# A spectral filter and MLP kernel: the first batch turned on TensorE in SBUF instead of through DRAM, and the stages of the later batches scheduled further ahead

## Chip, cores, metric

One core of one Trainium2 chip. The metric is the device time of one execution in microseconds (us), lower is better. The kernel before: 631.26 us, the median of 3 runs (625.03 to 633.33). Spans of a profiled execution ("the trace") are 1.7 to 2.0 us shorter than the same execution's device time. TensorE does the matmuls; the operand that stays in its array is called the weights, the other one moves. Its results land in the memory PSUM, from which VectorE or ScalarE copies them to the memory SBUF ("evicts" them). GpSimd copies within SBUF, and the DMAs move data to and from DRAM. "Granted clock" is the share of the full TensorE clock that the profile records as granted.

## The reference, cut to what matters

```python
X = np.fft.rfft(x, axis=1)                 # x: 8 batches x 3136 positions x 256 channels
y = np.fft.irfft(X * (filt_r + 1j*filt_i), n=3136, axis=1)
h = y.transpose(0, 2, 1) @ U @ V           # low rank over positions, rank 32
u = y + h.transpose(0, 2, 1)
out = u + np.maximum(u @ w_ch1, 0) @ w_ch2 # w_ch1: 256 x 1024, w_ch2: 1024 x 256
```

The Fourier transform over 3136 = 64 x 49 positions is done as matmuls in two steps with a filter product between the second step and its inverse. Between the steps rows and columns of the 64 x 49 arrangement have to change places.

## The kernel before

Each batch passes through `f1` (first transform), `mid` (second transform, filter product `uv`, its inverse), `low_rank`, and the output stage. An output group is 8 steps of the main loop; a batch is 6 groups or 48 steps. The change of places is done by writing a tile to DRAM (`ct1`, `ct2`) and reading it back in another order.

```python
def f1(u):                                        # cut
    ...   pf = w.T @ x ; asb = pf (evicted) ; store1: asb -> DRAM ct1

def mid(u):                                       # cut
    def do_i1(k, uv):
        pe = ps.tile([128, 2, DM], F32, tag="o" if u.n == 0 else "z", bufs=2)
        ...   pe = gz.T @ uv ; nc.scalar.copy(e, pe) ; e -> DRAM ct2
    for k in range(0, NK, 2):
        if u.n == 0 and i == 0:
            mirror_filters(c)                     # one part of the filters, 4 parts
        ...   a2 = load from ct1
        pz = ps.tile([128, 2, DM], F32, tag="z", bufs=2)
        nc.tensor.matmul(pz, wz[0], a2)
        nc.vector.tensor_mul(uv, pz, fab)
        if len(uvs) > 2: do_i1(*uvs.pop(0))       # 17 steps of this generator
        yield

def low_rank(u):  ...  load e2l and the tiles eb from ct2 ; ph = aus.T @ e

def stage4(gr):   ...  pu = eb.T @ sv ; ut = pu   # starts an output group
def mm1(gr, t):   ...  phh = w1.T @ ut ; h = relu(phh)
def mm2_part(gr, t): . pc += h.T @ w2 ; och = pc ; och -> out

for u in units[1:]:                               # steps, counted over all groups
    s = 48 * u.n                                  # u's own output starts at step s
    deal(f1s[u.n], 7, 2 if first else s - 62, 9 if first else s - 48)
    deal(mids[u.n], 17, 15 if first else s - 44, s - 11)
    for w in (s - 8, s - 6):
        plan[w].append(ranks[u.n])
```

Note for later: for every batch but the first, `pz` and `pe` share the two PSUM buffers of tag "z". The Tile scheduler places the instructions of each engine from this program; TensorE then takes its matmuls in that order: in the waits shown here no later matmul starts before the one that waits (6.6 us, below).

## Time and profile before

| stretch of the trace | us |
|---|---|
| start to the first `ut` eviction (the head) | 84.1 |
| first `ut` of a batch to first `ut` of the next: batches 0 to 6 | 73.5, 70.0, 71.5, 69.0, 65.6, 65.6, 62.3 |
| batch 7, without further transforms | 46.4 |
| last `ut` to the end | 19.5 |
| sum | 627.5 |

The `ut` eviction is the first VectorE instruction of an output group; its 49 start times cut the trace into comparable pieces. These periods are differences of those start times.

The busy tenths of the page in 40 slices of 15.7 us, for TensorE, for the granted TensorE clock and for the DMA engines:

```profile
PE   2145469997999979997999989999999999999996
PEclk9996669999899979999999999999999999999999
DMA  9768939528834587238834596338633663342112
```

TensorE is mostly idle in the first five slices; after that it is busy, with dips (a 7) at about 140, 220, 280 and 360 us.

Waits of TensorE, from the answer that lists who waited for whom (us in total, times, longest):

```profile
PE pu L425 <- DMA eb<-ct: 25.5, 6, 11.8
PE pz L339 <- DMA a<-ct: 17.9, 2, 16.6
PE pz L339 <- DVE uv L348: 13.0, 4, 4.3
```

Of the 25.5 us, 11.8 lie in the head; the other five waits are the dips. The head from VectorE's side, its timeline (start, duration, engine, line, what, how often, and in brackets the idle time before and who ended it):

```profile
35.93 4.62 DVE L348 TENSOR_TENSOR uv<-pz,fab 113x1024 f16<-113x1024 f32 x4 [16.08 <-PE pz L339]
40.58 0.69 DVE L196 COPY fab<-fab 64x2048 f16<-64x2048 f16 x1
44.67 4.62 DVE L348 TENSOR_TENSOR uv<-pz,fab 113x1024 f16<-113x1024 f32 x4 [3.41 <-ACT fab L197]
...
84.06 1.23 DVE L428 CAST ut<-pu 128x1024 f16<-128x1024 f32 x1 [9.79 <-PE pu L425]
```

Here the first batch waits for its own DRAM round trip (16.08 us), for a filter mirror in each quarter (3.41 us), and for the second round trip (9.79 us).

A piece of the period, all engines, lines of middle products and one `phh` only:

```profile
395.80 0.38 PE L339 MATMUL pz<-a,mats 98*128 98x512 f16 x1
...
396.02 0.59 PE L307 MATMUL pe<-uv,mats 113*98 113x512 f16 x2
...
396.65 0.58 ACT L318 CAST e<-pe 98x512 f16<-98x512 f32 x1
...
396.89 0.38 PE L438 MATMUL phh<-ut,w1sb 128*128 128x512 f16 x1
...
397.28 0.38 PE L339 MATMUL pz<-a,mats 98*128 98x512 f16 x1
```

A 512-column matmul at full clock lets the next one start after 0.216 us (`phh` to `phh` elsewhere).

### The profile page before, as it was taken

Reading aid. Unit: us, or ns where it says so; the run is one execution under the profiler, and the core shown is the slowest. Engines: PE = TensorE matmul, PEld = TensorE weight load, DVE = VectorE, ACT = ScalarE, POOL = GpSimd, SP = SyncE. Lnnn points to the kernel's source line nnn. Section 1 sums busy time; section 2 is a strip of 40 time slices with the busy share of each in tenths; the row PEclk is TensorE's granted clock in tenths of the full one; section 3 lists DMA queues with packets and bytes.
Section 4 is the critical chain, followed back from the end, with each engine's and each line's share of the span. In section 5 each row is a group of like instructions: output and inputs, shape, how many; then the busy total and the mean of one; then the engine's idle time right before and its main releaser. Section 6 shows DMA issues by size and latency. Waiting matters only on the chain.

```text
span 627.5 us, 11123 instructions
## 1 busy us (share of the span) xinstructions
PE 548.2 (87%) x4427; PEld 377.8 (60%) x4427; DVE 330.8 (53%) x351; ACT 340.4 (54%) x577; POOL 57.7 (9%) x76
## 2 busy tenths in 40 slices
PE   2145469997999979997999989999999999999996
PEld 1112237655766657665776757667766776677775
DVE  1247424694249543884259552975388536843331
ACT  1225236565555736565556745666566665656663
POOL 6379201000000000000000000000000000000000
PEclk9996669999899979999999999999999999999999
DMA  9768939528834587238834596338633663342112
GB/s 214 168 151 161 197 93 244 168 86 212 200 135 140 135 198 243 86 105 201 223 108 137 136 230 210 100 102 231 216 93 95 195 197 107 100 145 86 68 68 101
DMA packets 76868, 95.51 MB, mean 152 GB/s; under 512 B 6775, under 2 KB 60328, under 8 KB 76816
## 3 DMA queue, kind: packets, MB, share of 16 engines
q1 hardware_dynamic: 67440, 77.49, 39.8%
q0 software_dynamic: 7504, 15.91, 15.9%
q10 hardware_dynamic: 1872, 1.41, 0.7%
q8 instruction: 35, 0.57, 0.4%
q14 instruction: 17, 0.14, 0.1%
HBM read 59.10 MB, written 51.58 MB: 176 GB/s over the span
## 4 chain that ended last, share of the span: by engine, by line
PE 59%; DMA 7%; DVE 4%; ACT 3%; SPq 2%; issue 1%; ACTq 0%; DVEq 0%
PE pc L461 21%; PE phh L438 20%; PE pe L307 6%; PE pz L339 4%; DMA eb<-ct 4%; PE pu L425 3%; PE pc L466 3%; PE pf L254 2%; DMA ct<-e 2%; ACT h L440 2%; SPq L369 1%; DVE asb L269 1%; ACT e L318 1%; DMA e2l<-ct 1%; DVE uv L348 1%
## 5 line engine op out<-in xcount | busy, mean ns | idle before, releaser
L440 ACT ACTIVATE h<-phh 128x512 f16<-128x512 f32 x392 | 232.6, 598 | 161.4 <-PE phh L438 160.2
L461 PE MATMUL pc<-w2sb,h 128*128 128x256 f16 x1568 | 246.4, 275 | 0.0
L438 PE MATMUL phh<-ut,w1sb 128*128 128x512 f16 x784 | 243.7, 386 | 2.9 <-DVE ut L428 1.3
L461 PEld LDWEIGHTS <-h 128*128 128x128 f16 x1568 | 149.7, 98 | 82.1 <-issue 8.4
L348 DVE TENSOR_TENSOR uv<-pz,fab 113x1024 f16<-113x1024 f32 x128 | 153.3, 1220 | 42.6 <-PE pz L339 32.7
L472 DVE COPY och<-pc 128x512 f32<-128x512 f32 x98 | 67.2, 686 | 98.9 <-PE pc L466 96.0
L318 ACT CAST e<-pe 98x512 f16<-98x512 f32 x128 | 74.3, 585 | 76.3 <-PE pe L307 75.5
L438 PEld LDWEIGHTS <-w1sb 128*128 128x128 f16 x784 | 95.7, 146 | 18.8 <-issue 8.7
L428 DVE CAST ut<-pu 128x1024 f16<-128x1024 f32 x49 | 59.9, 1223 | 85.5 <-PE pu L425 85.3
L307 PE MATMUL pe<-uv,mats 113*98 113x512 f16 x240 | 77.3, 406 | 0.0
L339 PE MATMUL pz<-a,mats 98*128 98x512 f16 x120 | 47.3, 405 | 32.6 <-DMA a<-ct 17.9
L425 PE MATMUL pu<-sv,eb 96*128 96x64 f16 x768 | 36.2, 196 | 26.0 <-DMA eb<-ct 25.5
L425 PEld LDWEIGHTS <-eb 96*128 96x128 f16 x768 | 32.9, 99 | 40.5 <-issue 24.9
L466 PE MATMUL pc<-idn,ut 128*128 128x128 f16 x392 | 54.8, 221 | 0.0
L307 PEld LDWEIGHTS <-mats 113*98 113x98 f16 x240 | 30.5, 133 | 36.4 <-issue 25.7
L145 POOL DMA_DIRECT2D x<-in_x_dram x24 | 14.5, 626 | 340.7 <-PE pf L254 336.8
L466 PEld LDWEIGHTS <-ut 128*128 128x128 f16 x392 | 38.4, 98 | 9.1 <-issue 0.2
L254 PE MATMUL pf<-x,wf 128*128 128x256 f16 x192 | 33.0, 299 | 11.9 <-DMA x<-in_x_dram 11.7
L269 DVE CAST asb<-pf 128x1024 f16<-128x1024 f32 x21 | 25.7, 1224 | 21.0 <-PE pf L254 18.6
L365 DVE COPY eb<-h 32x2048 f16<-32x2048 f16 x32 | 19.9, 678 | 30.6 <-ACT h L398 30.6
L254 PEld LDWEIGHTS <-wf 128*128 128x128 f16 x192 | 18.7, 104 | 22.3 <-issue 13.6
L267 ACT CAST asb<-pf 128x1024 f16<-128x1024 f32 x21 | 21.2, 1012 | 15.8 <-DMA ct<-asb 7.6
(59 smaller groups left out, 133.5 us busy)
## 6 DMA issues: line engine op xcount, KB each, us to landing
out_dram<-och SPq DMA_DIRECT2D x48, 512.0 KB
ct<-e SPq DMA_DIRECT2D x64, 196.0 KB
x<-in_x_dram POOLq DMA_DIRECT2D x24, 512.0 KB, 6.7
eb<-ct SPq DMA_DIRECT2D x96, 128.0 KB
a<-ct SPq DMA_DIRECT2D x28, 392.0 KB
ct<-asb SPq DMA_DIRECT2D x42, 256.0 KB
a<-ct SPq DMA_DIRECT2D x4, 441.0 KB
ct<-asb SPq DMA_DIRECT2D x3, 288.0 KB
```

The lines of the kernel that those rows point to most:

```text
L254: nc.tensor.matmul(pf[:, (j if u.n == 0 else 2 * i + j), :], w, u.x[c][:, r, :], start=True, stop=True, skip_group_check=True)
L307: nc.tensor.matmul(pe[0:98, :, :], gz[0][f], uv[:, f, :, :], start=(f == 0), stop=(f == 1))
L318: nc.scalar.copy(e[:, i:i + 2, :], pe[0:98, :, :])
L339: nc.tensor.matmul(pz, wz[0], a2[c][:, i:i + 2, 0:DM], start=True, stop=True)
L348: nc.vector.tensor_mul(uv.rearrange("p f k d -> p f (k d)"), zin, fin)
L425: nc.tensor.matmul(pu[:, dh, 64 * i:64 * i + 64], e2[:, s, 128 * dh:128 * dh + 128], sv[:, 64 * r:64 * r + 64], start=(i == 0), stop=True, ...
L428: nc.vector.tensor_copy(gr.ut.rearrange("p h (c q s) -> p h c q s", q=64, s=2), pu.rearrange("p h (c s q) -> p h c q s", q=64, s=2))
L438: nc.tensor.matmul(ph, w1v[:, dh, :, t], gr.ut[:, dh, :], start=(dh == 0), stop=(dh == 1))
L440: nc.scalar.activation(h, ph, RELU)
L461: nc.tensor.matmul(o, gr.h[tt][:, i * 128:(i + 1) * 128], w2sb[:, tt * DM:(tt + 1) * DM], start=(tt == 0), stop=False, skip_group_check=True)
L466: nc.tensor.matmul(o[:, dh * 128:dh * 128 + 128], gr.ut[:, dh, i * 128:i * 128 + 128], idn, start=False, stop=(dh == 1), skip_group_check= ...
L472: nc.vector.tensor_copy(gr.och[:, 2 * y:2 * y + 2, :], gr.pc.rearrange("p (j d) -> p j d", j=2))
```

## The change

Intent: (1) the first batch computes its first transform channel-major (x is the stationary operand), so that the change of places can be done by matmuls against an identity (`turn1`, `turn2`) and stays in SBUF; its filters are all loaded at once, mirrored by three engines, and its rank sum is taken in the spectrum. (2) The stages of batches 2 to 7 come earlier: first transform by 16 to 18 steps, middle transform and rank step by 12.

The diff, cut to its core (`...` and "cut" mark what is left out):

```diff
+    xh = [sb.tile([128, NR, 64], F16, tag="och", bufs=2) for _ in range(2)]   # channel-major
+    uh = cst.tile([128, 2, 100, NK], F16)
+    for c in range(3): ...                                  # first transform, batch 0
+        nc.tensor.matmul(pf[:, j], u0.x[c][:, r, 128*dh:128*dh+128], wf[:, ...])
+        dst = xh[dh][:, 0:48].rearrange("p (h r) k -> p r h k", h=2)[:, r:r + 4]
+        (nc.scalar.copy if n_pf % 2 else nc.vector.tensor_copy)(dst, pf)
+    for c in range(3): ...                                  # the same for U: pu, into xhu
+    def rows_of(t, k):
+        return t.rearrange("p r k -> p (r k)")[:, k:k + 97 * 32 + 1:32]       # 98 columns, 64 bytes apart
+    def turn1(i):                                           # pa = xh turned, 4 matmuls
+        nc.tensor.matmul(pa[0:98, s, ...], rows_of(xh[dh], 2 * i + s), idn)
+        nc.scalar.copy(at[i], pa[0:98])
+    def u_turn(): ... nc.tensor.matmul(pt[0:98, k], rows_of(xhu, k), idn[0:32, 0:32])  # ptu, 32 of them
+    def i1_turned(i): ... nc.tensor.matmul(po[dh][...], uv[:, f, s, ...], gt[...][f])
+        nc.scalar.copy(uh[:, dh, :, 2*i-2:2*i+2], po[dh].rearrange("p k b -> p b k"))
+    def turn2(u, g): ... nc.tensor.matmul(pt[0:96, s, ...], uh[:, dh, b:b + 3]..., idn)  # 100 in all
 # cut: mirrors on VectorE, ScalarE and GpSimd; fab memset moved from GpSimd to VectorE;
 # cut: rank sum h_part from uv; all ct1/ct2 traffic of batch 0 removed
+    for g in range(1, 6):
+        deal(turn2(u0, g), 4, max(8*(g-1)-4, 0), 8*(g-1)+4)
     for u in units[1:]:
         s = 48 * u.n
-        deal(f1s[u.n], 7, 2 if first else s - 62, 9 if first else s - 48)
-        deal(mids[u.n], 17, 15 if first else s - 44, s - 11)
-        for w in (s - 8, s - 6): plan[w].append(ranks[u.n])
+        if u.n == 1: deal(f1s[1], 7, 0, 7); deal(mids[1], 17, 11, 37); rank = (38, 40)
+        else:
+            deal(f1s[u.n], 7, s - 78, s - 66)
+            deal(mids[u.n], 17, s - 56, s - 23)
+            rank = (s - 20, s - 18)
+            x_step[s - 92] = u
```

## The prediction

> **What bounds the kernel now.** Read from the busy times by window: until 84.1 us (the first `ut` eviction) TensorE works about 30 us for the first batch. From the timeline: `x` lands at 8.4 to 15 us; PE then sits idle 16.6 us for the `a` read-back; then four blocks of 8 to 9 us, each gated by a 1.91 us ScalarE filter mirror followed by four 1.15 us `uv` products; then 11.8 us for `eb<-ct`. After 84 us PE is 98 to 99% busy except near 140, 220, 280 and 360 us, where `pu` waits 2.8 to 3.7 us for `eb<-ct` and the granted clock dips afterwards. From one batch's first `ut` to the next's (6 groups): 73.5, 70.0, 71.5, 69.0, 65.6, 65.6 us. So 65.6 us is undisturbed, and some 17 us are lost in the first four: 13 in these waits, the rest mostly at half clock.
>
> **Head after the change.** No DRAM write and read-back, all filter loads queued at once. Estimated: `x` timing unchanged; 96 matmuls of 128 columns end near 19 to 20 us; first `uv` near 23.5 us (it waits for the first ScalarE mirror). Then VectorE is the pacer: 16 products x 1.15 to 1.22 + `aur` 1.2 + two `gb` 2.4 = 23 to 24 us. ScalarE is close behind: 16 `at` x 0.59, 16 `uh` about 0.5, four mirrors x 1.91, three big evictions 1.0 = 28 us from 21 us on. So the last `uv` ends near 47 to 50, then the rest of the inverse, rank sum, first turn, `put_h` and `pu` take 5 to 6 us. First `ut` near 54 us instead of 84: 30 us gained, all on the critical path. GpSimd's mirrors come behind 29 DMA issues of 0.6 us, ready at about 31 us, just in time.
>
> PE in this stage needs about 20 us at full clock but 36 at half. The Trainium skill, "TensorE: Matmul & The Clock Gate", Part 1, says that the array runs at 1.2 GHz until about 3.4 us of sustained activity; the trace agrees (512-column matmuls 0.43 us apart at 36 to 58 us, 0.22 just after). I expect it mostly warm after 30 us.
>
> **Steady part.** Added on PE: 100 turning matmuls of the second transpose. The skill (same page, weight-path perf modes) limits fast weight load to 128-column weights; these have 96: I estimate 0.055 to 0.08 us each, 5 to 8 us in all. Removed: most of the `eb` waits, since the rank step now comes 20 steps ahead instead of 8 (a step is 1.0 to 1.7 us, the loads took 6 to 8 us). Only batch 1 stays tight: its middle transform still ends at step 37 and its tiles are needed at step 44. I leave 8 us of residual waits and half clock of the 17.
>
> **Sum.** 627.5 - 30 - 17 + 8 + 7 = about 595 us in the trace; runs lie about 3 us above it: 598 us.
>
> Chances: faster over 2%: 0.95; within 2%: 0.04; slower: 0.01. Range 584 to 612.
>
> **Signs.** First `ut` at 50 to 59 us; batch periods near 66 us from the second on; the first 75 or more; no `pu<-eb` waits after batch 1; VectorE over 80% busy between 24 and 48 us; clock near full from 30 us.
>
> **What would make it wrong.** PE staying at half clock through the head (+10 us); ScalarE's 64-byte-strided `uh` writes costing much over 0.5 us; the GpSimd mirrors or filter loads arriving late; batch 1's round trips stalling more than 8 us.

## The result

The changed kernel takes 598.61 us, median of 4 runs (594.02 to 600.38), against 629.55 us of the kernel before (4 runs): ratio 0.950, 95% interval 0.941 to 0.959. A ratio here is the mean time of one kernel's fast runs over the mean of the other's fast runs of the same rounds, so it is not quite the ratio of the medians quoted beside it. Executions over 1.5% slower than the fastest of the same kernel are left out of the means. The total is within 1 us of the prediction. The pieces are not:

| stretch | before | predicted | after |
|---|---|---|---|
| head, to first `ut` | 84.1 | 54 | 73.4 |
| first `ut` to the end | 543.5 | 541 | 524.2 |
| of it: batch 0 | 73.5 | 75 or more | 83.1 |
| batches 1 to 6 | 70.0, 71.5, 69.0, 65.6, 65.6, 62.3 | near 66 | 60.3, 63.4, 63.5, 63.5, 63.4, 60.1 |
| span of the trace | 627.5 | 595 | 597.6 |

(541 is 595 less 54.) The head came out 19 us worse than predicted and the rest 17 us better; the right total is two errors that cancel. The experiments below look for both.

The same views after the change. The busy tenths:

```profile
PE   1698896899999999999999999999999999999996
PEclk9955889799999999999999999999999999999999
DMA  9859058558626974397439763756346642422112
```

TensorE is now busy in the head, but at a granted clock of 5 tenths in two slices; the dips later are gone except one at about 100 us. The waits for DMA of more than 1 us, besides that for x:

```profile
PE pu L251 <- DMA un<-in_moe_U_dram: 5.5, 1, 5.5
PE pz L306 <- DMA a<-ct: 6.6, 1, 6.6
```

The first is in the head, the second is the dip at 100 us. The waits of `pu` for `eball` (the old `eb`), 25.5 us before, are 0.3 us in all. The head from VectorE's side:

```profile
28.02 1.22 DVE L317 TENSOR_TENSOR uv<-pz,fab 113x1024 f16<-113x1024 f32 x1 [3.29 <-ACT fab L206]
33.33 2.36 DVE L317 TENSOR_TENSOR uv<-pz,fab 113x1024 f16<-113x1024 f32 x2 [4.09 <-PE pz L306]
...
53.55 3.56 DVE L317 TENSOR_TENSOR uv<-pz,fab 113x1024 f16<-113x1024 f32 x3 [5.09 <-PE pz L306]
...
73.44 1.23 DVE L561 CAST ut<-pu 128x1024 f16<-128x1024 f32 x1 [0.41 <-PE pu L558]
```

VectorE, predicted as the pacer, waits for TensorE's `pz`. Busy time in the stretch of the middle transform (columns: us, then busy us and count of TensorE, weight loads, VectorE, ScalarE, GpSimd; granted clock; DMA share and GB/s):

```profile
20.00:40.00 20.00, 18.23 (x119) 15.46 (x117) 9.01 (x12) 11.45 (x18) 18.43 (x22) 0.67 0.78 112
40.00:60.00 20.00, 17.42 (x132) 13.36 (x131) 10.43 (x11) 15.72 (x22) 7.50 (x8) 0.59 0.72 135
```

TensorE is busy 35.65 of 40 us (89%), VectorE 19.44 (49%). What TensorE does there, from its timeline:

```profile
33.09 0.80 PE L269 MATMUL pa<-mats,xh 128*98 128x128 f16 x4
...
34.74 2.85 PE L277 MATMUL ptu<-mats,eball 32*98 32x32 f16 x16
...
38.67 0.87 PE L328 MATMUL po<-mats,uv 113*128 113x100 f16 x8
39.34 1.55 PE L269 MATMUL pa<-mats,xh 128*98 128x128 f16 x8
```

The start-to-start times of successive matmuls (medians) are 0.167 us for both `pa` and `ptu`, though one moves 128 columns and the other 32. The clock does not matter to `pa` either: from 44.0 to 47.4 us, at full granted clock, they are still 0.167 us apart. That points to a stream bound by its weight loads (tested below with h1, h2 and h4): `pa` and `ptu` are the two that take their weights from `xh` or `xhu` with 64 bytes between columns. `po`, with contiguous weights, is at 0.081 in the half-clock stretches.

The steady part after the change, the same group of lines as before (from the period of batch 4):

```profile
364.85 0.38 PE L306 MATMUL pz<-a,mats 98*128 98x512 f16 x1
...
365.07 0.60 PE L423 MATMUL pe<-uv,mats 113*98 113x512 f16 x2
...
365.71 0.58 ACT L434 CAST e<-pe 98x512 f16<-98x512 f32 x1 [0.55 <-PE pe L423]
...
367.83 0.38 PE L306 MATMUL pz<-a,mats 98*128 98x512 f16 x1
```

The next `pz` comes 1.5 us after the end of the `e` eviction and starts on time. Call a matmul late when it starts more than 0.09 us after the usual start-to-start time for the width of the matmul in front of it. Per batch, this lateness adds up to 3.7 us before (period of batch 4) and 1.6 us after; the difference is the 2.1 us between 65.6 and 63.5. Of it, 1.5 us are the starts of `pz` (2.1 us before, 0.6 after).

### The profile page after: what moved, and what is told of

It is laid out like the page before. It is cut to its first block, busy times and chain, and to the rows that moved or that the text cites. A ratio compares the mean times of both kernels' runs of the same rounds, so it can differ in the third digit from the quotient of the medians.

```text
span 597.6 us, 11827 instructions
## 1 busy us (share of the span) xinstructions
PE 559.9 (94%) x4775; PEld 407.7 (68%) x4775; DVE 347.3 (58%) x370; ACT 356.8 (60%) x608; POOL 46.5 (8%) x68
## 4 chain that ended last, share of the span: by engine, by line
PE 78%; DMA 8%; ACT 6%; POOL 3%; issue 3%; DVE 2%; SPq 0%; ACTq 0%; POOLq 0%
PE pc L594 26%; PE phh L571 26%; PE pe L423 7%; PE pz L306 4%; PE pu L558 4%; PE pc L599 3%; DMA un<-in_moe_U_dram 2%; PE pf L391 2%; ACT asb L394 2%; DMA x<-in_x_dram 1%; ACT e L434 1%; DMA ct<-al 1%; DMA a<-ct 1%; PE pt L506 1%; PE ph L527 1%
## 5 line engine op out<-in xcount | busy, mean ns | idle before, releaser
L594 PE MATMUL pc<-w2sb,h 128*128 128x256 f16 x1568 | 240.4, 273 | 0.0
L434 ACT CAST e<-pe 98x512 f16<-98x512 f32 x112 | 65.0, 586 | 48.5 <-PE pe L423 47.4
L561 DVE CAST ut<-pu 128x1024 f16<-128x1024 f32 x49 | 59.8, 1221 | 11.1 <-PE pu L558 10.9
L423 PE MATMUL pe<-uv,mats 113*98 113x512 f16 x210 | 62.5, 378 | 0.2
L599 PE MATMUL pc<-mats,ut 128*128 128x128 f16 x392 | 54.1, 220 | 0.0
L306 PE MATMUL pz<-a,mats 98*128 98x512 f16 x105 | 39.4, 383 | 8.0 <-DMA a<-ct 6.6
L558 PEld LDWEIGHTS <-eball 96*128 96x128 f16 x768 | 29.8, 98 | 12.2 <-issue 3.9
L461 DVE COPY eball<-h 32x2048 f16<-32x2048 f16 x34 | 22.1, 680 | 21.8 <-ACT h L488 18.4
L423 PEld LDWEIGHTS <-mats 113*98 113x98 f16 x210 | 25.3, 124 | 12.8 <-issue 5.1
L558 PE MATMUL pu<-sv,eball 96*128 96x64 f16 x768 | 31.6, 194 | 0.7 <-DMA eball<-ct 0.3
L391 PE MATMUL pf<-x,wf 128*128 128x256 f16 x168 | 25.8, 275 | 1.1 <-DVE ut L561 0.3
```

The lines of the kernel that those rows point to most:

```text
L306: nc.tensor.matmul(pz, wz[0], a2, start=True, stop=True)
L391: nc.tensor.matmul(pf[:, j], wf[:, 128 * (8 * c + r):128 * (8 * c + r) + 128], u.x[c][:, r, :], start=True, stop=True, skip_group_check=True)
L423: nc.tensor.matmul(pe[0:98, :, :], gz[0][f], uv[:, f, :, :], start=(f == 0), stop=(f == 1))
L434: nc.scalar.copy(e[:, i:i + 2, :], pe[0:98, :, :])
L558: nc.tensor.matmul(pu[:, dh, 64 * i:64 * i + 64], e2[:, s, 128 * dh:128 * dh + 128], sv[:, 64 * r:64 * r + 64], start=(i == 0), stop=True, ...
L561: nc.vector.tensor_copy(gr.ut.rearrange("p h (c q s) -> p h c q s", q=64, s=2), pu.rearrange("p h (c s q) -> p h c q s", q=64, s=2))
```

## The experiments

In the tables "head" is the first `ut`; "batch 0" and "later" are periods as above. "Ratio" is against the kernel before in the same rounds, with 95% interval. Traced spans are single executions. All results were correct. Throughout, TensorE matmuls are told apart by their PSUM tile.

### The two parts apart: s1_sched_only, s2_turn_only

s1 is the kernel before with this edit:

```diff
-        deal(f1s[u.n], 7, 2 if first else s - 62, 9 if first else s - 48)
-        deal(mids[u.n], 17, 15 if first else s - 44, s - 11)
-        for w in (s - 8, s - 6):
+        deal(f1s[u.n], 7, 2 if first else s - 78, 9 if first else s - 66)
+        deal(mids[u.n], 17, 15 if first else s - 56, s - 11 if first else s - 23)
+        for w in ((s - 8, s - 6) if first else (s - 20, s - 18)):
-            x_step[s - 76 if u.n > 2 else s - 74] = u
+            x_step[s - 92] = u
```

> The kernel before with only the new schedule of batches 2 to 7; the first batch still goes through DRAM. Theory A (the schedule carries most of the gain, because the turned first batch gives its shorter head back in the first period): first ut stays at 84 us, the six-group periods from the second on fall from 70.0, 71.5, 69.0, 65.6, 65.6, 62.3 to about 60 to 64, total about 604 us. Rival B (the recorded prediction: the turning gains about 22 us net, the schedule about 9): about 618 us.

s2 is the changed kernel with the reverse edit for batches 2 to 7.

> The changed kernel with the old schedule of batches 2 to 7. Theory A: first ut at 73 us as in the changed kernel, but the later periods go back to about 70, 71, 69, 65.6, so about 620 us. Rival B: about 606 us.

| kernel | median us | ratio | span | head | batch 0 | batches 1 to 6 |
|---|---|---|---|---|---|---|
| before | 630.0 | 1 | 627.5 | 84.1 | 73.5 | 70.0, 71.5, 69.0, 65.6, 65.6, 62.3 |
| s1 schedule only | 601.44 | 0.955 (0.949 to 0.961) | 600.0 | 85.3 | 74.0 | 59.8, 63.5, 63.5, 63.5, 63.5, 60.1 |
| s2 turned batch only | 629.36 | 0.990 (0.978 to 1.002) | 631.1 | 72.1 | 84.5 | 70.9, 70.7, 71.3, 67.7, 65.6, 62.3 |
| after, both | 598.61 | 0.950 (0.941 to 0.959) | 597.6 | 73.4 | 83.1 | 60.3, 63.4, 63.5, 63.5, 63.4, 60.1 |

Two of the four runs of s2, the profiled one among them, counted as slow; its ratio uses the fast two, its periods are only shown for their pattern. Theory A held: the schedule alone brings almost everything. From s1 to after, the traces lose 11.9 us in the head (85.3 to 73.4) and get 9.1 us back in batch 0 (74.0 to 83.1). The turning nets about 2.4 us of trace, where the prediction had 23 (30 less about 7). Single traces scatter here: s3 and s4 below have the same head and the same batch 1, and their head and batch 0 together are 150.5 and 153.4 us, against 156.5 in after and 159.3 in s1. So the net of the turning lies between 2 and 9 us, far from 23 in any case.

### Where the 2.1 us per period come from: s3_shift8, s4_shift4, s6_f1_late

Three versions of the changed kernel, with only this edit:

```diff
-            deal(f1s[u.n], 7, s - 78, s - 66)    # s6: s - 72, s - 60
-            deal(mids[u.n], 17, s - 56, s - 23)  # s3: s - 52, s - 19   s4: s - 48, s - 15
-            rank = (s - 20, s - 18)              # s3: (s - 16, s - 14) s4: (s - 12, s - 10)
```

> The changed kernel, with the middle transform and rank step of batches 2 to 7 only 8 steps further ahead than before, not 12. A group is 8 steps, so this keeps the old place of the middle transforms within a group. Theory P (the 2.1 us per period by which the undisturbed periods fell, 65.6 to 63.5, come from where in the group the middle transforms fall): periods of 65.6 us and no waits for eball. Rival Q (they come from the longer lead): 63.5 us or close.

> The changed kernel with the middle transform and rank step of batches 2 to 7 only 4 steps ahead of the old place: the new place within the group, but little lead. Theory P: undisturbed periods of 63.5 us, with some waits for eball of 0 to 3 us in the early batches. Rival Q: 65 us or more in undisturbed periods.

| kernel | median us | ratio | undisturbed period | spread of the 17 `pz` | steps from first to middle transform | matmuls late, sum per period |
|---|---|---|---|---|---|---|
| before | | 1 | 65.6 | 24.7 us | 4 | 3.7 us |
| s6 | 610.18 | 0.975 (0.969 to 0.981) | 64.7 | 28.7 | 4 | 2.8 |
| after | 598.61 | 0.950 (0.941 to 0.959) | 63.5 | 32.3 | 10 | 1.6 |
| s3 | 595.13 | 0.946 (0.940 to 0.952) | 63.5 | 33.6 | 14 | 1.6 |
| s4 | 596.11 | 0.945 (0.936 to 0.955) | 62.8 | 41.4 | 18 | 1.1 |

Theory P fell: with the old place in the group (s3) the period stays 63.5. Rival Q, the lead by itself, fell too: with the least lead (s4) the period is the shortest. What orders all five rows is the spread of the middle products, which gave theory R, tested with s6:

> The changed kernel with the first transform of batches 2 to 7 six steps later (steps s-72 to s-60), everything else as it is: only 4 steps between it and the middle transform, as in the kernel before. Theory R (the 2.1 us per undisturbed period come from this distance: with 4 steps the read-back tiles a come late, and the 17 middle products are squeezed into about 25 us where VectorE cannot keep up, which costs TensorE a bubble of about 0.18 us at most pz): periods back to about 65.5 us, pz spread over about 25 us, no eball waits. Rival Q (lead alone): 63.5 us as in the changed kernel. Total by R about 608 us, by Q about 598 us.

R held in direction and a little over half in size: the period went from 63.5 to 64.7, not 65.5, because the products were squeezed into 28.7 us rather than 25. Why the same 4 steps gave 24.7 us in the kernel before stays open. The expectation also named the wrong engine. In the period before, 11 of the 17 `pz` start 0.05 us after an `e` eviction of ScalarE ends, and 4 of them (two counted in both) 0.05 us after a `uv` of VectorE; in s4 none does. `pz` and `pe` take turns in two PSUM buffers, and a `pz` that has to follow closely waits until the other engine has emptied one. So: when the read-back tiles come late in the program, the scheduler puts the 17 products close together, and TensorE loses about 0.17 us at most `pz`. In s4, where most are 2.5 us or more apart, no `pz` is late. That the two PSUM buffers are the reason is read from which eviction ends just before; no run gave `pz` and `pe` separate buffers. The total of s6 also holds waits of 9.0 us for `a<-ct` in batch 0's period (88.6 us), so its total says less than its later periods.

### Batch 0's period: s5_mid1_15

```diff
-            deal(mids[1], 17, 11, 37)
+            deal(mids[1], 17, 15, 37)
```

> The changed kernel with the middle transform of batch 1 starting at step 15 instead of 11 (still ending at 37). Theory: the 6.6 us wait of pz for a<-ct in the first period, which blocks all of TensorE's in-order stream, and the half clock after it go away: first period about 76 us instead of 83, total about 591 us. Rival: the tighter middle transform moves the stall to the VectorE-bound products and the eball loads of batch 1, total within 2 us of 598.

Measured: 591.37 us, ratio 0.945 (0.939 to 0.951); batch 0 76.0 us instead of 83.1. This looks as if the theory held, but the other traces do not bear it out. The wait that is left in s5, then that of s3, which has not this edit, then that of c2 (below), which has it:

```profile
PE pz L306 <- DMA a<-ct: 3.2, 1, 3.2
PE pz L306 <- DMA a<-ct: 2.8, 1, 2.8
PE pz L311 <- DMA a<-ct: 6.4, 1, 6.4
```

In the changed kernel TensorE reached `pz` before the last store of the first transform had landed (7.8 us) and been read back (6.3 us), and everything behind `pz` in its order stood still: 6.6 us, and half clock for some microseconds after. The edit did not move this `pz`: TensorE comes to it 26.9 us after the first `ut` in after and 26.7 us in s5 (26.3 to 27.2 in all traces with the turned first batch). What differs is when the read-back could be issued: 24.4 to 26.1 us after the first `ut` in the traces with a wait under 4 us, 26.3 to 27.1 in the others. Without the edit the wait was 1.8 to 6.7 us and batch 0 took 75.5 to 84.5 us (88.6 in s6, with a second such wait); with it, in s5, c1, c2 and c3, 3.2 to 6.4 us and 75.5 to 79.0 us. The ratio of s5 is that of s3 (0.946) and s4 (0.945). So the wait, with the half clock after it, does make batch 0 longer, but that the four steps shortened it is not shown. The prediction had looked for this batch's stall at the `eball` loads of step 44; there it was 0.3 us.

### The head: h1_contig98, h2_contig128, h4_runs16

h1 stores `xh` as 32 blocks of 98 contiguous columns, so the weights of `turn1` and `u_turn` are read contiguously and the eviction writes scattered elements (cut: the same for `xhu` and the last columns, and the order of `pf`):

```diff
-    xh = [sb.tile([128, NR, 64], ...)]
+    xh = [sb.tile([128, NK, 98], ...)]
-                dst = xh[dh][:, 0:48].rearrange("p (h r) k -> p r h k", h=2)[:, r:r + 4]
+                dst = xh[dh][:, :, 0:96].rearrange("p k (h c) -> p h c k", h=2)[:, :, 2 * r:2 * r + 8]
-        return t.rearrange("p r k -> p (r k)")[:, k:k + 97 * 32 + 1:32]
+        return t[:, k]
```

> The changed kernel with the turned first transform stored so that the weights of the first turn lie contiguous (98 columns side by side instead of 64 bytes apart); the evictions write the stride instead. Theory L (the head is bound by TensorE, which loads the strided weights at 0.17 to 0.18 us each): pa drops from 0.17 to about 0.11 us apart and ptu from 0.18 to about 0.09, 7 us less TensorE time, first ut near 67 us instead of 73.4, total about 592 us. Rival M (the head is bound by DMA landing, mirrors and the ScalarE/VectorE chain): spacing falls or not, first ut stays within 1.5 us of 73.

h2 in addition loads 128 columns each time (30 more, results unused):

```diff
-        return t[:, k]
+        return t.rearrange("p k c -> p (k c)")[:, 98 * k:98 * k + (128 if k < NK - 1 else 98)]
```

> As h1_contig98, but each weight load of the first turn takes 128 columns (30 more, whose results nobody reads), so that fast weight load as the skill states it can apply. Theory L with it: ptu falls further, to about 0.03 to 0.06 us, pa stays at the 0.107 of a half-clock 128-column matmul or falls to 0.056 if the denser stream warms the clock; first ut 62 to 66 us, total 587 to 592 us. Rival M: first ut within 1.5 us of 73. If the column count does not matter, the same as h1_contig98.

| kernel | median us | ratio | head | `pa` us apart | `ptu` us apart | one `xh` eviction on ScalarE |
|---|---|---|---|---|---|---|
| after | 598.61 | 0.950 | 73.4 | 0.167 | 0.167 | 0.6 us |
| h1 | 611.21 | 0.977 (0.970 to 0.985) | 89.5 | 0.107 | 0.084 | 2.5 us |
| h2 | 613.01 | 0.978 (0.971 to 0.985) | 90.2 | 0.106 | 0.027 | 2.5 us |
| h4 | 587.24 | 0.930 (0.924 to 0.936) | 65.1 | 0.080 | 0.026 | 0.5 us |

The `pa` of h4 are a mixture of 0.107 us at half clock and 0.056 at full. h1 and h2 did to TensorE what was expected and lost 16 to 17 us of head all the same, which neither theory had foreseen. The reason is on one line of h1's ScalarE timeline:

```profile
20.24 14.98 ACT L240 CAST xh<-pf 128x512 f16<-128x512 f32 x6
```

The changed kernel's evictions of the same size, from the same view:

```profile
20.34 2.21 ACT L239 CAST xh<-pf 128x512 f16<-128x512 f32 x4
```

2.5 us each against 0.55 (the stretch divided by the count; a single record reads 2.96 and 0.58). The write of single 2-byte elements 196 bytes apart takes about five times as long as runs of 64 elements; the evictions on VectorE went from 0.69 to 2.5 us and more. h4 keeps h2's layout and lets the eviction run in the other order, so that it writes 8 neighbouring elements (16 bytes) and takes the stride on the PSUM side:

```diff
-                dst = ....rearrange("p k (h c) -> p h c k", h=2)[:, :, 2 * r:2 * r + 8]
-                src = pf.rearrange("p h r (j k) -> p h (r j) k", j=2)
+                dst = ....rearrange("p k (h c) -> p h k c", h=2)[:, :, :, 2 * r:2 * r + 8]
+                src = pf.rearrange("p h r (j k) -> p h k (r j)", j=2)
```

> As h2_contig128 (contiguous weights, 128 columns a load), but the evictions of the first transform write 8 neighbouring elements (16 bytes) at a time and read PSUM with the stride instead. Theory L2 (h1 and h2 lost 16 us only because 2-byte writes 196 bytes apart made each eviction 2.5 us instead of 0.6; TensorE's weight loads do bind the head): evictions back at 0.6 to 0.8 us, ptu at 0.03 us and pa at 0.11 us or less, first ut at 63 to 67 us instead of 73.4, total 588 to 592 us. Rival M (TensorE is not what binds the head): evictions at 0.6 to 0.8 us but first ut within 1.5 us of 73. If strided PSUM reads cost as much as the strided writes did: evictions stay at 2 us or more and first ut near 89 us.

```profile
19.91 3.11 ACT L240 CAST xh<-pf 128x512 f16<-128x512 f32 x6
```

0.52 us each, and 0.69 on VectorE as in the changed kernel, so the strided PSUM read is free here. TensorE in h4, where 18 `ptu` take 0.71 us (16 took 2.85):

```profile
31.33 0.71 PE L280 MATMUL ptu<-mats,eball 32*128 32x32 f16 x18
31.97 0.61 PE L272 MATMUL pa<-mats,xh 128*128 128x128 f16 x4
```

Theory L2 held: the head is 8.3 us shorter although x landed 0.8 us later in this trace (first matmul at 9.7 us against 8.9); the evictions and the total came out slightly better than expected. Rival M fell: TensorE did bind the head, through its weight loads. The gain lies wholly after the first `uv`: from there to the first `ut` it is 37.5 us against 45.4. Part of this may be the clock, since h4 was granted full clock for 19.1 us of that stretch and after for 13.7. At equal clock, 17.1 us in both, s4 takes 43.8 us and c2 (which has h4's layout) 37.1, so about 6.7 us are the layout alone.

### All parts, and the rest of the head: c1_all, c2_u_early, c3_warm

c1 is h4 with s5's and s4's schedule.

> h4_runs16 with the middle transform of batch 1 from step 15 and those of the later batches 8 steps later (the places of s4_shift4). If the three parts add up: first ut as in h4_runs16, first period about 76 us, later undisturbed periods 62.8 us: total about 578 to 582 us, faster than both kernels. If the shorter head only moves the wait to the first period (its DMAs start earlier but weights and x land no sooner), the first period grows by what the head lost and the total stays near 586.

c2 is c1 with the loads of `un` and `ul` issued ahead of the last two loads of x, because TensorE's order has U matmuls in the middle of the first transform and stood 4.4 to 5.5 us waiting for `un`.

> c1_all with the two loads of U issued ahead of the last two loads of x, so that the U matmuls, which stand ahead of the last third of the first transform in TensorE's order, no longer hold it up for 5 us. Theory U: first transform ends about 2 us earlier (x itself must still land), first ut near 63 us, total about 580 us. Rival: the mirrors and filter loads set the pace after it, first ut within 0.7 us of 65.0.

c3 is c1 with 16 unneeded matmuls in that gap:

```diff
+        if c == 1:
+            warm = ps.tile([128, 512], F32, tag="w", bufs=1, name="warm")
+            for j in range(16):
+                nc.tensor.matmul(warm, u0.x[1][:, j % 8, 0:128], wf[:, 0:512], ...)
+            nc.vector.tensor_copy(wsb, warm[:, 0:2])
```

> c1_all with 16 matmuls of 512 columns that nobody needs, on data of the second x tile, in the 5 us in which TensorE waits for the third; the scheduler then also puts the U matmuls behind the first transform. Theory W (half clock is a large part of what the head costs over the recorded prediction): matmuls of the last third of the first transform at 0.056 us apart instead of 0.107, first ut at 60 to 62 us. Rival: spacing falls but the ScalarE and VectorE evictions and the filter mirrors pace the head by now; first ut no earlier than in c2_u_early.

| kernel | median us | ratio | head | x landed | head less x | batch 0 |
|---|---|---|---|---|---|---|
| after | 598.61 | 0.950 (0.941 to 0.959) | 73.4 | 8.9 | 64.5 | 83.1 |
| h4 | 587.24 | 0.930 (0.924 to 0.936) | 65.1 | 9.7 | 55.4 | 80.4 |
| c1 | 583.73 | 0.927 (0.922 to 0.931) | 65.0 | 9.6 | 55.4 | 75.5 |
| c2 | 584.23 | 0.931 (0.925 to 0.936) | 63.9 | 9.4 | 54.5 | 79.0 |
| c3 | 579.91 | 0.926 (0.921 to 0.930) | 60.5 | 7.5 | 53.0 | 75.5 |

When the first tile of x lands varies from trace to trace (7.3 to 10.2 us) for reasons outside the edits, so heads are compared from there. Even so they scatter: the six traces with the changed kernel's head (after, s2 to s6) have 62.8 to 67.4 us, and single differences below 5 us of this column show nothing. The part from x to the first `uv` is steadier: 18.1 to 19.1 us in those six, 18.0 in h4, 18.4 in c1, 17.5 in c2 and 15.9 in c3. From the first `uv` on, h4, c1, c2 and c3 are alike (37.0 to 37.5 us).

c1: the head of h4 and the later periods of s4 add up, with 62.8 us in the undisturbed later periods; batch 0 took 75.5 us, which for the reason given under s5 is not to be put down to s5's edit. Its trace is 581.8 us, at the upper end of what was expected, because batch 0 and one later period kept small waits (3.8 us for `a<-ct`, 1.8 for `eball`). c2: the wait for U fell to 0.9 us, but the part up to the first `uv` gained only 0.5 to 0.9 us, no more than the scatter: theory U is not shown, and the total did not move. c3: the last third of the first transform runs at full clock,

```profile
15.82 1.06 PE L233 MATMUL pf<-wf,x 128*128 128x128 f16 x16
```

against 1.87 us for 16 in c1:

```profile
20.38 1.87 PE L233 MATMUL pf<-wf,x 128*128 128x128 f16 x16 [0.18 <-ACT xh L240]
```

and the part from x to the first `uv` is 1.6 us shorter than in c2, where the U wait is nearly gone too. Theory W is right in kind and small in size for this stretch; the first `uv` of c3 then waits 4.0 us for a filter load. The clock falls back to half at about 23 us, when TensorE next waits, so c3 does not test what full clock through the whole head would give. c3 has the lowest median of all, 579.91 us, but its ratio is that of c1 within the noise.

## Why the prediction was right and wrong

**Right in the total, 598.0 predicted and 598.61 measured, by two errors that cancel.** The range and the direction were right. The pieces:

1. *"First `ut` near 54 us instead of 84: 30 us gained"* is wrong: 73.4 us. The step that failed is *"Then VectorE is the pacer"*. The load of strided weights by 64 `pa` and 32 `ptu` stands in none of its terms. Measured, each costs 0.167 us, at half and at full clock alike, 16 us for all 96, where the columns alone would give 64 x 0.107 + 32 x 0.027 = 7.7 us at half clock. h4 removed this and got 9.1 us of head, counted from the landing of x.
2. *"I expect it mostly warm after 30 us"* is wrong: the granted clock was 0.50 at 30 to 40 us and 0.59 on average at 40 to 60 us, with TensorE 87 to 91% busy by the records. The prediction's own list of dangers had "PE staying at half clock through the head (+10 us)". c3 shows some of its cost (1.6 us in the first transform). For the rest the traces give a hint: with the same head, the stretch from the first `uv` to the first `ut` took 49.1 us with 3.4 us at full granted clock (s3), 45.0 to 45.4 with 13.7 (after, s2, s5, s6) and 43.8 with 17.1 (s4), about 0.4 us less for each microsecond at full clock (time before the first recorded change is counted as half, as the spacing of the matmuls says). Drawn out to full clock throughout, this estimate gives some 9 us, but it lies far outside what was measured, and with h4's layout (17.1 to 20.5 us at full clock) no such slope shows.
3. Not foreseen: TensorE's order put U's matmuls before the last third of the first transform (5.5 us wait, but worth at most 0.9 us when taken away in c2, which is within the scatter).
4. Cut at the first `uv`, the 19.4 us are 4.5 before it (28.0 us, predicted 23.5) and 14.9 after it (45.4 us, predicted 30.5). Of the 14.9, h4 took back 7.9, of which the layout alone is about 6.7. Some 7 us after the first `uv` stay open; half clock in the middle transform and the waits of 4 to 5 us before `pz`, still there in h4, are the candidates that the traces show. No run separates them.
5. *"65.6 us is undisturbed"* is wrong, and it is the main step that failed in the other direction. Those periods held 3.7 us of late matmul starts that no idle column shows. The new schedule took 2.1 us out of each (s1, with the old first batch, has the same 63.5), s4 2.8 us. The prediction expected "batch periods near 66 us".
6. *Removed: most of the `eb` waits* was right: 25.5 us became 0.3 us. s2 with the old schedule has 13.8 us of them (in a run counted as slow).
7. *"Only batch 1 stays tight"* was right in the batch and wrong in the place: 6.6 us for `a<-ct` at the start of its middle transform, 0.3 us for its tiles at the end. Whether s5 helped this wait is not shown.
8. *100 turning matmuls at 0.055 to 0.08 us, 5 to 8 us in all*: the 79 pairs of successive records in the trace have a median of 0.057 us, 5.7 us for 100, at the low end. The Trainium skill, "TensorE: Matmul & The Clock Gate", section "Weight-path perf modes — Fast Weight Load (FWL) and DoubleRow", restricts the fast load to 128-column weights. This agrees with h1 and h2 (98 columns 0.084 us apart, 128 columns 0.027), but with 128 moving columns no cost of the load of 96 contiguous columns shows: 0.057 us is what 128 columns take with other weights too (0.056).
9. The share-out of the gain was wrong altogether: the prediction gave the turning about 23 us net (30 less 7) and the schedule about 9; the traces say 2.4 us (s1 to after; 2 to 9 with the scatter) and 27.5 us (before to s1).

## What to carry to other kernels

Two orders of the same work can both show an engine 99% busy and differ by 3%: compare the start-to-start times of its instructions with what they take undisturbed, above all where tiles share a few PSUM buffers, and leave a load issued from DRAM enough steps that its users need not be bunched. Price a transposing matmul by its weight load as well as by its moving columns, and choose the layout so that neither the weight load nor the eviction that produces it goes element by element with a stride (2 bytes in every 64 or 196 here); h4 did both by moving the stride to the PSUM side of the eviction. When a total comes out as predicted, check the pieces before believing the reasons. And before a shorter wait is put down to an edit, look at the same wait in the traces that do not have the edit.

## What the Trainium skill lacked or had wrong

- "Advanced Engine Details and Errata", section "Memory Cachelines", says that SBUF has 16-byte lines and that at least two hits on a line are needed for full speed. The runs agree and give the cost, which the page does not: weight loads of 98 columns with one column per line 0.167 us (at half and at full clock), contiguous 0.084 us (at half clock); evictions writing one 2-byte element per line 2.5 us for 512 elements, in runs of 8 elements 0.52 us. Runs of 4 elements (8 bytes, the `uh` evictions) took 0.49 us for 400 elements, so four hits were enough; two were not tried.
- The same section says of PSUM that non-contiguous patterns slow down matmuls and that every two consecutive elements should be contiguous; it does not say what this means for evictions. For reads of PSUM no such cost showed: 512 elements of 4 bytes, neighbours 128 bytes apart, 0.52 us on ScalarE (h4), against 0.55 us in the changed kernel, and 0.69 us on VectorE in both.
- "TensorE: Matmul & The Clock Gate", section "LDWEIGHTS (loading the stationary operand)", gives columns / 1.2 in ns. At half clock this fits (98 / 1.2 = 82 ns, measured 84). At full clock 96 columns must take no more than the 57 ns measured between the `pt` matmuls, less than the page's 80.
- The same page, Part 1, has the clock rise after about 3.4 us of sustained activity. In the changed kernel TensorE was busy without a gap in the records from 30 to 40 us and the granted clock stayed 0.50. The page does not say how busy an array bound by its weight loads counts (Part 4 says so only of matmuls in transpose mode, which these are not); the runs do not settle it either.
- No page: the granted clock that the profile shows is 1.00 until the first change that it records. In the changed kernel's window from 20 to 25 us it reads 1.00 while, up to 23.4 us, 128-column matmuls start 0.107 us apart, half speed. The spacing is the better witness there.
